# A new opening, a later fourth batch and a fourth buffer for scaled q in a cosformer-attention and expert-mixture kernel

## The chip, the cores and the metric

The kernel runs on one core of one Trainium2 chip. The metric is device time in microseconds (us) of one execution. Executions are compared within rounds on the same chip; a run over 1.5% above the fastest of its kernel counts as slow and is left out of a ratio. Engines are named as in the profile: PE is the matmul engine, DVE the vector engine, ACT the scalar engine, POOL and SP the two from which the transfers here are issued ("POOLq", "SPq"). A lower-case q at the end of a name in the wait views means that engine's sequencer. The granted PE clock is the share of its full clock that the matmul engine was given: 1.00 is full, 0.50 half.

## The reference

Eight batches of linear attention feed a dense mixture of eight experts, whose weights per token come from eight Sinkhorn iterations. Cut to what matters:

```python
batch, n_heads, seq, head_dim = 8, 8, 576, 64         # q, k, v in float32
q_p = phi(q, cos_w, sin_w)    # relu(q), once times cos and once times sin: 128 features
k_p = phi(k, cos_w, sin_w)
kv  = einsum('bhsf,bhsd->bhfd', k_p, v)
z   = sum(k_p, axis=2)
attn = einsum('bhsf,bhfd->bhsd', q_p, kv) / (einsum('bhsf,bhf->bhs', q_p, z)[..., None] + 1e-06)
x = attn as (4608, 512)                                # tokens by model width
P = sinkhorn(exp(x @ w_gate), 8 rounds)
out = sum over e of P[:, e:e+1] * (relu(x @ w1[e]) @ w2[e])
```

## The kernel before

The first 163 us are the subject. They are cut into blocks. In block j, PE runs the first expert's feed-forward layers for token block j (8 slots of first-layer tiles, 8 of second-layer tiles), and between them, slot by slot, the attention of a later batch: sums of batch j+1 (k times v), its denominators, spreading of reciprocals and numerators. In the same block DVE and ACT prepare batch j+2, and POOL issues the loads of batch j+3.

The pools that the change touches:

```python
ld      = pool("ld", bufs=4)          # loads of q, k, v; every name has its own four buffers
qp_pool = pool("qp_pool", bufs=3)     # q times cos and sin, read by the transpose
rb_pool = pool("rb_pool", bufs=4)     # reciprocals spread over partitions
```

From batch 2 on, scaled q is turned by a DMA transpose that the sync queue issues (four per batch, numbered here (batch, hk), where hk is one of four pairs of heads). A q buffer is free again only when its transpose has landed (DVE stands 1.23 us for one at 82.01, below):

```python
def prep_q(b, hk):
    q16 = loaded.pop(("q", b, hk))
    by_dma = b >= 2
    ...                                               # ReLU on DVE
    q_p = qp_pool.tile([P, C, 2, D], F16, name="q_p")
    ve.tensor_tensor(out=q_p[:], in0=q16..., in1=cs, op=ALU.mult)
    if by_dma:
        qTs[b, hk] = q_pTs[(b * HK + hk) % len(q_pTs)]
        turned = nc.sync.dma_start(out=qTs[b, hk], in_=q_p[:]..., transpose=True)
        if b == 3 and hk == 0:
            after(landing["v", b, 1], turned)         # a wait for the last v load of its batch
```

Loads are issued on POOL. `held_back` makes a load wait for the DVE instruction that stands last before it in the program, so it cannot go out before DVE has come that far:

```python
def load(b, half, names="qkv", held_back=False):
    for name in names:
        x = ld.tile([P, 2, C, D], F16, name=f"{name}_ld")
        i = nc.gpsimd.dma_start(out=x[:]..., in_=view[:, 2 * half : 2 * half + 2])
        if held_back:
            after(ve.last, i)
```

The table that deals work to slots, cut to blocks 1 and 2 and the loads:

```python
(4, prep_q, 0), (5, prep_q, 1), (8, prep_k, 0), (8, prep_q, 2), (9, prep_k, 1), (10, prep_kv, 0), ...   # j == 1
(4, prep_q, 0), (5, prep_k, 0), (5, prep_q, 1), (6, prep_k, 1), (8, prep_q, 2), ... (11, prep_kv, 0)    # j == 2
if j == 1:
    at(j, 15, sums, b + 1, 0)
    at(j, 12, load, b + 2, half, name, True)          # batch 4: all six loads
elif j and b + 2 < B:
    at(j, 11 + half, load, b + 2, half, "qkv", True)  # batches 5 to 7: behind DVE's v copy of (b+1, 0)
```

`prep_kv` is the scaled product of k and the copy of v.

## Time and profile before

| | |
|---|---|
| time | 975.6 us median of 3 (975.55 to 975.99) |
| profiled run, one more | 973.88 us, span 972.1 us, mean granted PE clock 0.999 |
| PE busy | 959.4 us, so 12.7 us idle |
| starts of blocks 1, 2, 3 and 4 on PE | 44.86, 67.08, 85.62, 104.65 us |

Each row of a timeline gives start, length, engine, source line (a helper's), operation, what is written and read, and in brackets how long the engine had been idle and what ended that. For a DMA the length is that of its issue, not of its transfer. First the sync queue, asked for batch 4's four transposes one by one:

```profile
76.03 1.61 SPq L392 DMA_TRANSPOSE q_pT<-q_p  x1
77.75 3.07 SPq L392 DMA_TRANSPOSE q_pT<-q_p  x1
80.92 1.31 SPq L392 DMA_TRANSPOSE q_pT<-q_p  x1
82.83 1.27 SPq L392 DMA_TRANSPOSE q_pT<-q_p  x1
```

DVE at the last of them, POOL at the first of batch 5's loads, and the landing of the fourth transpose:

```profile
82.01 0.76 DVE L109 TENSOR_TENSOR q_p<-q_ld,acc_hi 128x1152 f16<-128x1152 f16 x1 [1.23 <-DMA q_pT<-q_p]
...
83.35 0.45 DVE L109 COPY acc_lo<-v_ld 128x576 f16<-128x576 f16 x1
```

```profile
84.10 0.72 POOL L233 DMA_DIRECT2D q_ld<-in_q_dram  x1 [13.47 <-DVE acc_lo L109]
```

```profile
DMA to landing us min/median/max: 4.2/4.2/4.2
```

What to see: with three buffers the fourth product of q has to wait until the first transpose has landed (1.23 us). DVE's v copy comes after that product, and it is the v copy that releases batch 5's loads (84.10). So the fourth transpose (82.83) is out 1.27 us ahead of them, and it lands in 4.2 us. And PE in block 3, from the denominators of batch 4 to the first spread of block 3:

```profile
91.43 0.84 PE L109 MATMUL small_ps<-q_pT,zsel 128*32 128x192 f16 x24
92.20 1.04 PE L109 MATMUL h_ps<-xT,w1e 128*128 128x512 f16 x4
93.07 0.65 PE L109 MATMUL small_ps<-wg,xT 128*128 128x8 f16 x20
93.58 1.89 PE L109 MATMUL h_ps<-xT,w1e 128*128 128x512 f16 x8
95.30 0.41 PE L109 MATMUL small_ps<-hl,acc_hi 96*128 96x192 f16 x3
```

### The profile page before, as it was taken

The numbers are of one execution on the slowest core, as the hardware profiler recorded it, in microseconds if no ns is written. First come the engines' busy times: TensorE is split into PE (matmuls) and PEld (weight loads), VectorE is DVE, ScalarE is ACT, GpSimd is POOL, SyncE is SP. The second block draws the span as 40 slices with busy tenths as digits, with TensorE's granted clock in tenths as the row PEclk, the third lists the DMA queues.
The fourth block names the chain that finished last, engine by engine and source line by source line (L and its number), as shares of the span: only waits on it lengthen the run. The fifth ranks groups of instructions, "written<-read, shape, count | busy, mean of one in ns | idle before, by whom it ended". The sixth has DMA issues, their size and how long they took to land.

```text
span 972.1 us, 20258 instructions
## 1 busy us (share of the span) xinstructions
PE 959.4 (99%) x7855; PEld 674.6 (69%) x7855; DVE 807.4 (83%) x1831; ACT 565.0 (58%) x1264; POOL 60.7 (6%) x82
## 2 busy tenths in 40 slices
PE   9999999999999999999999999999999999999997
PEld 6545555567777777777777777777777777777775
DVE  7767776789898887987888987987888987987887
ACT  5767665577776555555555555555555555555551
POOL 6231210010000000000000000000000000000001
PEclk9999999999999999999999999999999999999999
DMA  9999988231004301332004301322004401115435
GB/s 162 188 154 173 156 137 184 44 69 50 26 26 93 69 25 50 68 62 57 25 26 93 69 25 51 68 54 65 26 25 86 75 25 42 33 28 124 123 90 127
DMA packets 81200, 74.72 MB, mean 77 GB/s; under 512 B 33360, under 2 KB 73040, under 8 KB 81104
## 3 DMA queue, kind: packets, MB, share of 16 engines
q0 software_dynamic: 27232, 30.94, 20.4%
q1 hardware_dynamic: 53632, 42.24, 17.8%
q8 instruction: 61, 1.00, 0.4%
q14 instruction: 35, 0.29, 0.1%
q10 hardware_dynamic: 240, 0.26, 0.1%
HBM read 84.30 MB, written 12.98 MB: 100 GB/s over the span
## 4 chain that ended last, share of the span: by engine, by line
PE 91%; DMA 4%; issue 2%; DVE 1%; POOL 1%; ACT 0%; POOLq 0%; DVEq 0%; SPq 0%; ACTq 0%
PE rows_ps L109 34%; PE h_ps L109 28%; PE p_ps L109 11%; PE copied_ps L109 11%; PE y_ps L109 4%; PE small_ps L109 3%; DMA k_ld<-in_k_dram 1%; DMA w1e<-in_moe_w_dram 1%; DMA w2e<-in_moe_w_dram 1%; DVE acc_hi L975 0%; POOL q_ld L233 0%; POOL hs_last L990 0%; DMA out_dram<-acc_lo 0%; DVE H L905 0%; DVE S L203 0%
## 5 line engine op out<-in xcount | busy, mean ns | idle before, releaser
L975 DVE SCALAR_TENSOR_TENSOR acc_lo<-rows_ps,P_tok,acc_lo 128x512 f32<-128x512 f32 (+1 forms) x322 | 203.8, 642 | 74.9 <-PE rows_ps L109 74.8
L109 PEld LDWEIGHTS <-H 128*128 128x128 f16 x2080 | 203.1, 98 | 82.3 <-issue 1.4
L911 ACT CAST u<-h_ps 128x384 f16<-128x384 f32 x288 | 137.5, 478 | 129.7 <-PE h_ps L109 129.7
L109 PEld LDWEIGHTS <-w1e 128*128 128x128 f16 x1632 | 157.7, 98 | 67.2 <-issue 5.3
L905 DVE CUSTOM_DVE_ANT_0 H<-p_ps,u 128x384 f16<-128x384 f32 x329 | 181.7, 552 | 7.2 <-PE p_ps L109 7.1
L109 PEld LDWEIGHTS <-hs 128*128 128x128 f16 x1500 | 146.6, 98 | 56.2
L109 PE MATMUL p_ps<-xT,T 128*128 128x384 f16 x672 | 164.2, 326 | 1.0 <-DVE H L905 0.9
L109 PE MATMUL h_ps<-S,w1e 128*128 128x384 f16 x672 | 164.2, 326 | 0.8 <-ACT u L911 0.6
L109 PE MATMUL rows_ps<-V,H 128*128 128x256 f16 x1000 | 150.0, 273 | 0.7 <-DVE acc_hi L975 0.7
L109 PE MATMUL rows_ps<-w2e,hs 128*128 128x256 f16 x1000 | 150.0, 273 | 0.0
L109 PE MATMUL h_ps<-xT,w1e 128*128 128x384 f16 (+1 forms) x616 | 148.8, 351 | 0.1
L943 ACT ACTIVATE H<-h_ps 128x384 f16<-128x384 f32 x144 | 70.6, 490 | 94.5 <-PE h_ps L109 94.5
L109 PEld LDWEIGHTS <-T 128*128 128x128 f16 x1008 | 98.4, 98 | 31.9 <-issue 4.9
L109 PE MATMUL rows_ps<-w2e,H 128*128 128x256 f16 (+1 forms) x568 | 94.4, 285 | 0.0
L924 ACT COPY copied_ps<-h_ps 128x384 f32<-128x384 f32 x144 | 67.5, 469 | 36.0 <-PE h_ps L109 35.2
L934 ACT ACTIVATE H<-copied_ps 128x384 f16<-128x384 f32 x144 | 70.8, 492 | 20.4 <-PE copied_ps L109 20.4
L109 PE MATMUL h_ps<-S,T 128*128 128x384 f16 x336 | 81.8, 325 | 0.6 <-ACT copied_ps L109 0.5
L109 PE MATMUL copied_ps<-xT,w1e 128*128 128x384 f16 x336 | 82.1, 326 | 0.0
L109 PE MATMUL copied_ps<-w2e,H 128*128 128x256 f16 x504 | 75.6, 273 | 0.0
L109 PE MATMUL rows_ps<-V,hs 128*128 128x256 f16 x500 | 75.0, 273 | 0.0
L975 DVE SCALAR_TENSOR_TENSOR acc_lo<-copied_ps,P_tok,acc_lo 128x256 f32<-128x256 f32 x126 | 60.3, 479 | 0.4
L975 DVE SCALAR_TENSOR_TENSOR acc_hi<-rows_ps,P_tok,acc_hi 128x512 f32<-128x512 f32 (+1 forms) x56 | 41.4, 739 | 20.6 <-PE rows_ps L109 19.7
(146 smaller groups left out, 947.7 us busy)
## 6 DMA issues: line engine op xcount, KB each, us to landing
S<-x_saved SPq DMA_DIRECT2D x114, 192.0 KB, 2.4
out_dram<-acc_lo SPq DMA_DIRECT2D x62, 128.0 KB, 2.4
w1e<-in_moe_w_dram POOLq DMA_DIRECT2D x7, 1024.0 KB, 8.8
w2e<-in_moe_w_dram POOLq DMA_DIRECT2D x7, 1024.0 KB, 9.6
q_ld<-in_q_dram POOLq DMA_DIRECT2D x16, 288.0 KB, 6.5
k_ld<-in_k_dram POOLq DMA_DIRECT2D x16, 288.0 KB, 7.8
v_ld<-in_v_dram POOLq DMA_DIRECT2D x16, 288.0 KB, 9.6
x_saved<-S SPq DMA_DIRECT2D x12, 192.0 KB, 1.8
```

Source lines behind the costliest of these rows:

```text
L109: i = getattr(self.engine, name)(*args, **kwargs)
L905: latest = ve._custom_dve(TENSOR_ADD_SAT, out=out, in0=ps[:, 0:TU], in1=t[:], s0=FP32_MAX, s1=0.0)
L911: se.copy(out=t[:], in_=ps[:, 0:TU])
L924: se.copy(out=Y[:, 0:TU], in_=X[:, 0:TU])
L934: se.activation(out=h11, in_=Y[:, 0:TU], func=AF.Relu)
L943: se.activation(out=h12, in_=X[:, 0:TU], func=AF.Relu)
L975: ve.scalar_tensor_tensor(out=a, in0=rows, scalar=P_tok[:, g, self.e : self.e + 1], in1=a, op0=ALU.mult, op1=ALU.add,)
```

## The change

The intent: shorten the opening, where PE runs fillers; take away the wait of PE at 59 us on ACT; let scaled q of a batch go ahead without waiting for its own transposes (a fourth buffer, paid with one of the reciprocals'); and keep the DMA transposes of batch 3 away from its loads, by holding them for v and holding batch 4's loads for the transposes. The core of the diff, with cuts marked:

```diff
-        qp_pool = ... bufs=3            # scaled q
+        qp_pool = ... bufs=4
-        rb_pool = ... bufs=4            # reciprocals
+        rb_pool = ... bufs=3
-        def load(b, half, names="qkv", held_back=False):
+        def load(b, half, names="qkv", held_back=False, behind=None):
-                if held_back:
+                if behind is not None:
+                    after(turnings[behind], i)
+                elif held_back:
                     after(ve.last, i)
 # opening
         load(0, 0, "q")
+        load(0, 1, "q")
         ...iota...
+        load(0, 0, "k")
         ...
-        load(0, 1, "q")
-        for name in "kv":
-            load(0, 0, name)
-            load(0, 1, name)
+        load(0, 1, "k")
+        for half in range(2):
+            load(0, half, "v")
 ... (filler of half width; memsets moved ahead; all k products behind the key sums;
 ...  spreads and numerators of batch 0 between the first feed-forward matmuls;
 ...  half of the sums of batch 3 moved from the end of block 1 into block 2)
 # transposes of batch 3
-                if b == 3 and hk == 0:
+                if b == 3:
                     after(landing["v", b, 1], turned)
+                turnings[b, hk] = turned
 # block 1 and block 2
-                    (4, prep_q, 0), (5, prep_q, 1), (8, prep_k, 0), (8, prep_q, 2),
-                    (9, prep_k, 1), (10, prep_kv, 0), (10, prep_k, 2), (12, prep_q, 3),
-                    (12, prep_kv, 1), (12, prep_k, 3), (13, prep_kv, 2), (14, prep_kp, 3), ...
+                    (4, prep_q, 0), (5, prep_q, 1), (9, prep_k, 0), (8, prep_q, 2),
+                    (10, prep_k, 1), (12, prep_q, 3), (12, prep_k, 2), (13, prep_k, 3),
+                    (13, prep_kv, 0), (14, prep_kv, 1),
-                    (4, prep_q, 0), (5, prep_k, 0), (5, prep_q, 1), (6, prep_k, 1),
-                    (8, prep_q, 2), (8, prep_k, 2), (10, prep_q, 3), (10, prep_k, 3), ...
+                    (5, prep_q, 0), (6, prep_q, 1), (8, prep_k, 0), (8, prep_q, 2),
+                    (9, prep_k, 1), (10, prep_q, 3), (10, prep_k, 2), (11, prep_k, 3), ...
-                if j == 1:
-                    at(j, 15, sums, b + 1, 0)
-                        at(j, 12, load, b + 2, half, name, True)
+                        at(j, 12, load, b + 2, half, name, True, (b + 1, HK - 1))
```

## The prediction

> **What bounds the kernel now.** I read the page's first and fourth parts, then PE's own waits in the opening 90 us, then time-ordered views of PE, DVE and ACT where PE waits, and last the landings of the DMA transposes.
>
> ```profile
> PE 959.4 (99%) x7855; PEld 674.6 (69%) x7855; DVE 807.4 (83%) x1831; ACT 565.0 (58%) x1264; POOL 60.7 (6%) x82
> PE 91%; DMA 4%; issue 2%; DVE 1%; POOL 1%; ACT 0%; POOLq 0%; DVEq 0%; SPq 0%; ACTq 0%
> ```
>
> PE is busy in 959.4 of 972.1 us, so all idle PE time together is 12.7 us, 1.3% of the span. No reordering can win 2% (19.5 us) unless it also removes PE work. What is left is idle time and filler matmuls in the opening. PE's waits between 20 and 90 us:
>
> ```profile
> PE small_ps L109 <- ACT rb L109: 1.1, 1, 1.1
> PE small_ps L109 <- ACT acc_lo L109: 0.7, 1, 0.7
> PE small_ps L109 <- ACT q_pT L109: 0.4, 1, 0.4
> PE small_ps L109 <- DVE acc_hi L109: 0.3, 1, 0.3
> ```
>
> From about 86 us the stretches are full. In order of time on PE:
>
> ```profile
> 1.14 5.72 PE L109 MATMUL y_ps<-ones_sq 128*128 128x128 f16 x74 [1.14 <-DVE ones_sq L109]
> 7.65 0.34 PE L109 MATMUL small_ps<-ident,q_p 128*128 128x128 f16 x3 [0.29 <-DVE q_p L109]
> 16.54 1.15 PE L109 MATMUL y_ps<-ones_sq 128*128 128x512 f16 x5
> 17.67 0.42 PE L109 MATMUL small_ps<-hl,acc_hi 96*128 96x192 f16 x3
> 32.82 1.03 PE L109 MATMUL small_ps<-acc_lo,k_p 64*128 64x65 f16 x54 [0.73 <-ACT acc_lo L109]
> 33.78 1.04 PE L109 MATMUL y_ps<-w2e,hT 128*128 128x512 f16 x4
> 59.48 0.46 PE L109 MATMUL small_ps<-hl,acc_hi 96*128 96x192 f16 x3 [1.11 <-ACT rb L109]
> ```
>
> Matmuls on ones_sq are filler: they look busy, but PE is waiting. So up to 17.67 us the end is set by loads and DVE, not by PE. The DVE chain there:
>
> ```profile
> 4.32 0.50 DVE L109 COPY cs_half<-acc_hi 64x18 f16<-64x18 f16 x2 [1.39 <-ACT acc_hi L109]
> 6.83 0.77 DVE L109 TENSOR_TENSOR q_p<-q_ld,acc_hi 128x1152 f16<-128x1152 f16 x1
> 10.50 0.53 DVE L109 TENSOR_SCALAR k_ld<-k_ld 128x576 f16<-128x576 f16 x2 [1.57 <-DMA k_ld<-in_k_dram]
> 15.50 1.35 DVE L109 RECIPROCAL den<-y_ps 96x192 f32<-96x192 f32 x1
> ```
>
> The gap at 59.48 starts on ACT, which stands on a ReLU of the fourth batch's k until its load lands, with a copy to rb behind it:
>
> ```profile
> 57.89 0.68 ACT L109 ACTIVATE k_ld<-k_ld 128x576 f16<-128x576 f16 x1 [2.25 <-DMA k_ld<-in_k_dram]
> 58.48 0.57 ACT L109 COPY acc_lo<-y_ps 128x512 f32<-128x512 f32 x1
> 58.95 0.70 ACT L109 COPY rb<-small_ps 128x384 f32<-128x384 f32 x2
> ```
>
> [...] here sixteen take 3.59 us from 44.86, or 224 ns[...]. [...] the transpose issued at 53.64 us amid the batch's loads landed after 10.2 us, the one at 63.16, after the last v, after 3.3 us.
>
> **The change part by part.**
>
> Opening. The second q load and one k load are issued ahead of the other set-up work, so the index row is some 0.75 us later (one load's issue on POOL is 0.72 to 0.87 us). The two sines follow and end near 5.05 us instead of 4.29. But DVE now does its memsets (0.43 for the mask, about 0.4 for the rest) in the wait it had (1.39 us), and the cs_half copies (0.50) come after two q products. Then come the row reduction, select and spread (5.34 to 6.60 before), so the first q product starts at about 6.1 instead of 6.83. The four q products and the copies end at about 9.5, ahead of k, whose first half landed at 10.48 and, issued slightly earlier, may land at 10.2.
>
> From k's landings: ReLU of two k tiles 0.52; the second pair lands at about 11.9 and is ready near 12.5; key sums on PE 0.75, to 13.3; DVE's scaled k product (0.7) overlaps; mask product 0.3, to 13.75; denominators 0.5, to 14.35; one k product to 14.4; reciprocal 1.35, cast and remainder 0.7: about 16.5. Before, two more k products lay ahead of the reciprocal, and it ended at 17.60. Gain here 1.1 us, and the filler ahead (18 quarters before, 20 after) still covers the wait.
>
> From there PE runs four spreads and four numerators (0.36 each), the second half of the sums (0.65) and sixteen feed-forward matmuls (3.45), about 7.4 us with small filler: the next feed-forward tile starts at about 24.0 instead of 24.98.
>
> Then DVE binds. The changed order puts all four k products of batch 1 behind the last xT product (about 23.0); DVE had done two of them in its gaps before. Work from there: 4 k products and 4 q products at 0.69 (5.5), 2 ReLUs (0.6), 4 evictions of turned q at 0.46 (1.85), and 4 v copies at 0.38 (1.5), of which ACT did two before. That is 9.5 us, to 32.5; sums follow, and the second-layer tile starts at about 33.0 instead of 33.78. So of 1.1 us about 0.75 survives.
>
> Block 1 (second token block), where batch 2 is attended. The ReLU of k of batch 3 (the fourth batch) goes one slot later, behind the first attend. The rb copy then finds ACT free. PE needs, between 58.20 and 60.54, only 0.72 us for the spread and numerators that it took 2.34 us for: gain 1.62 us. The first half of the batch's sums (0.67 us at 66.41) moves into the next block, neutral. The scaled k and v copies move behind it: from about 64.3 DVE has 4 times 1.07 us to do, ending near 68.4; the sums in slot 2 reach the fourth tile at about the same time: at most 0.2 us.
>
> Block 2. All four transposes of this batch now wait for v (before, one of them went early, 53.64). With steps of 1.4 us from 62.0 and 3.4 to land, the last lands near 69.7, and batch 4's loads, which went out at 66.33, wait for that. An unhindered first load took 4.8 us (issued 84.1), so q is in at about 74.5. DVE reaches its first q product at 73.4 and stands about 1.1 us; three of them (1.0 each) end at 77.65, ahead of two xT products that free the accumulators of the third spread, due on PE at 77.75. The first is free at about 78.1: a loss of 0.4 to 0.6 us, taken as 0.5.
>
> The buffers: a fourth scaled q means its product doesn't wait for the transpose three products back (only 1.2 us of such DVE wait in the whole trace); three reciprocals suffice, since no more than two are outstanding when the next spread starts. Nothing for either. From block 3 on, order and engines' work are the same.
>
> Sum: 0.75 + 1.62 - 0.5 = 1.87, so 975.6 - 1.9 = 973.7 us.
>
> **Rivals.**
> (a) The later loads of batch 4 give it all back. For it: q, k and v land 2 to 3 us later than before, and ACT's ReLUs of k come ahead of output copies. Against: k moves from slots 5, 6, 8, 10 to 8 to 11[...]. If block 2 loses 2 us: 975.2 us.
> (b) The DVE queue of the opening isn't the bound I make it and all 1.1 us, or more, survives. Before, PE lost 0.40, 0.35 and 0.73 us at 29 to 33 us, part to ACT's v copies, now gone. Against: DVE's 9.5 us has no slack in my count. If right, with 1 us more: 972.6 us.
> [...]
> (d) A mere shift: the opening's gain is eaten by batch 2's loads (landing 36 to 43 us). Against: their issue waits only for earlier transfers and buffers, and PE is full from 33.78 to 44.86. It would leave 1.1 us: 974.5 us.
>
> **Range and chances.** The opening may bring 0.3 to 1.8, block 1 1.2 to 1.7, block 2 from 0.2 gained to 1.8 lost. Adding one bad term to otherwise central ones gives 971.5 to 975.5 us for 8 in 10. Faster by over 2% would need more idle time than there is: 0.01. Slower by over 2% would need a new wait of 19 us: 0.005. Within 2%: 0.985.
>
> **What would show it.** In the changed profile: first q product on DVE near 6.1; remainder done near 16.5; PE without waits from there to about 26, then two waits of 0.3 to 0.7 us on DVE among the turned q tiles; second-layer tile near 33.0. The 1.11 us wait on rb gone, and the 2.25 us ACT idle with it. All transposes of the fourth batch after v, 3 to 4 us each, then q loads near 69 (less the shift of 0.75); a DVE wait on q of about 1 us and a PE wait of about 0.5 us near 77. From block 3 on, everything the same but earlier by 1.9 us. I am wrong if PE shows a new wait of over 1 us in blocks 1 to 3, or if the second-layer tile starts before 32.3 or after 33.6.

Cut from it is what no trace of this case had shown: statements on the matmul clock, on matmul rates (the "sixteen" left standing are 512-column matmuls), on the order of work on ACT and on transfer engines; the second argument against rival (a); and rival (c), on the clock in the opening. That a block's feed-forward matmuls are a floor rested on the second and was not shown. No term of the sum is cut: 0.75 + 1.62 - 0.5 = 1.87 us, so 973.7 us.

## The result, and the profile after

The changed kernel took 983.77 us (median of 4, 981.29 to 984.21), the kernel before 975.63 us (975.55 to 975.99). The ratio is 1.0077, with a 95% interval of 1.006 to 1.0095; here and below a ratio is the mean time of one kernel's fast runs over the mean of the other's fast runs in the same rounds, so not quite the ratio of the medians quoted. The kernel became 0.8% slower: within the 2% that counts as the same, but slower where a small gain, to 973.7 us, had been predicted.

The profiled run took 984.03 us, with a span of 982.3 us. Busy time, from the page:

```profile
PE 961.8 (98%) x7886; PEld 674.9 (69%) x7886; DVE 808.9 (82%) x1834; ACT 564.0 (57%) x1261; POOL 60.4 (6%) x82
```

PE is busy 2.4 us longer (961.8 against 959.4) and idle 7.8 us longer (20.5 against 12.7); together that is the 10.2 us that the span grew. (The medians are only 8.1 us apart: the profiled run of the kernel before, 973.88 us, was faster than its median.) The first two blocks did what the change was for: PE starts blocks 1, 2 and 3 at 43.64, 63.40 and 84.04 us, that is 1.22, 3.68 and 1.58 us earlier than before (0.67 us of the 3.68 is work that was moved from block 1 to block 2). But block 4 starts at 114.59, 9.94 us later than before. So nearly everything that was lost was lost in block 3. The longest of PE's waits between 20 and 125 us (waited for: us in total, times, longest); the others are of 0.4 us and less:

```profile
PE small_ps L109 <- DMA q_pT<-q_p: 8.5, 2, 8.3
...
```

PE in order of time, the same work as in the lines of before from 91.43 to 95.30:

```profile
90.01 0.51 PE L109 MATMUL small_ps<-q_pT,zsel 128*32 128x192 f16 x12
90.75 0.35 PE L109 MATMUL small_ps<-q_pT,zsel 128*32 128x192 f16 x6 [0.22 <-DMA q_pT<-q_p]
99.36 0.51 PE L109 MATMUL small_ps<-q_pT,zsel 128*32 128x192 f16 x6 [8.27 <-DMA q_pT<-q_p]
99.81 1.89 PE L109 MATMUL h_ps<-xT,w1e 128*128 128x512 f16 x4
101.49 0.72 PE L109 MATMUL small_ps<-wg,xT 128*128 128x8 f16 x20
102.07 3.34 PE L109 MATMUL h_ps<-xT,w1e 128*128 128x512 f16 x8
105.24 0.41 PE L109 MATMUL small_ps<-hl,acc_hi 96*128 96x192 f16 x3
```

Two losses stand in these lines. The last quarter of batch 4's denominators waits 8.27 us for a transposed q. And the twelve feed-forward matmuls behind that wait take nearly twice as long: with the gate matmuls between them, from the row at 99.81 to the spread at 105.24 it is 5.43 us, where before it was 3.10 us (92.20 to 95.30). The stretches of 5 us show why; the columns are the stretch, busy time of PE, PEld, DVE, ACT and POOL, the granted PE clock, and the DMA share and rate:

```profile
95.00:100.00 5.00, 0.64 (x7) 0.27 (x7) 0.09 (x1) 0.00 (x0) 0.00 (x0) 0.50 0.80 131
100.00:105.00 5.00, 5.00 (x31) 2.04 (x30) 4.79 (x10) 1.31 (x3) 0.00 (x0) 0.50 0.07 14
```

The clock fell to half during the wait and stayed there until about 105 us: the trace's clock records have 0.50 from 94.79 to 105.03 us. PE had waited 8.27 us, and while the clock is 0.50 there is a 512-column matmul every 0.42 us (99.81 to 101.49 is four of them) instead of every 0.22 (92.20 to 93.07 in the kernel before, at 1.00). Block 3 is 11.52 us longer than before (30.55 against 19.03): 8.49 of waits, 2.33 of half-clock matmuls, and 0.70 spread over the denominators and the sums.

Why did the transpose come so late? The sync queue, transpose by transpose, and POOL's first load of batch 5:

```profile
74.80 2.50 SPq L403 DMA_TRANSPOSE q_pT<-q_p  x1
77.41 5.95 SPq L403 DMA_TRANSPOSE q_pT<-q_p  x1
83.46 1.60 SPq L403 DMA_TRANSPOSE q_pT<-q_p  x1
85.17 2.36 SPq L403 DMA_TRANSPOSE q_pT<-q_p  x1
```

```profile
83.50 0.72 POOL L234 DMA_DIRECT2D q_ld<-in_q_dram  x1 [10.01 <-DVE acc_lo L109]
```

The landing of the fourth transpose, asked for that transpose alone:

```profile
DMA to landing us min/median/max: 14.2/14.2/14.2
```

And DVE at the product and the copy that stood at 82.01 and 83.35 before:

```profile
78.47 0.76 DVE L109 TENSOR_TENSOR q_p<-q_ld,acc_hi 128x1152 f16<-128x1152 f16 x1
...
82.75 0.45 DVE L109 COPY acc_lo<-v_ld 128x576 f16<-128x576 f16 x1 [2.85 <-DMA v_ld<-in_v_dram]
```

The reader is to see an order that turned round. Batch 4's loads go out at 69.18 to 72.73 instead of 66.33 to 69.88, so its transposes are issued among them; the issue of the second alone occupies the sync queue for 5.95 us. DVE no longer notices: with a fourth buffer it makes its fourth q product at 78.47 without waiting for any transpose, and goes on to the v copy, which v's own landing (82.72) holds until 82.75. That copy releases batch 5's six loads at 83.50, while the third transpose is just being issued and the fourth has 1.7 us to go. The fourth goes out at 85.17 among these loads. The six land between 88.96 and 99.20 us, the fourth transpose at 99.32. With no loads in flight a transpose lands in 3.3 to 3.7 us (the first three of batch 3, issued at 60.58 to 63.41, land 3.31 to 3.37 us later, the fourth, issued at 64.91, 3.7 us later).

So the theory is: a transpose that is issued behind the first of a batch's loads lands late, in the change only when the last of the six has landed (the third transpose, issued 0.04 us ahead of the first of them, landed at 90.70); before, three buffers kept the transpose ahead of the next batch's loads without anybody having asked for it; the fourth buffer took that away. The rivals: that the hold on batch 4's loads alone does it, by making everything of batch 4 late; that the new order of work does it; and that the half clock has another cause than the wait.

### The profile page after: what moved, and what is told of

Read it like the earlier page. It is cut to its first block, busy times and chain, and to the rows that moved or that the text cites. A ratio compares the mean times of both kernels' runs of the same rounds, so it can differ in the third digit from the quotient of the medians.

```text
span 982.3 us, 20307 instructions
## 1 busy us (share of the span) xinstructions
PE 961.8 (98%) x7886; PEld 674.9 (69%) x7886; DVE 808.9 (82%) x1834; ACT 564.0 (57%) x1261; POOL 60.4 (6%) x82
## 4 chain that ended last, share of the span: by engine, by line
PE 93%; DMA 3%; DVE 2%; ACT 1%; issue 1%; POOL 0%; POOLq 0%; ACTq 0%; DVEq 0%; SPq 0%
PE rows_ps L109 34%; PE h_ps L109 28%; PE p_ps L109 11%; PE copied_ps L109 11%; PE y_ps L109 5%; PE small_ps L109 3%; DMA q_pT<-q_p 1%; DMA k_ld<-in_k_dram 1%; ACT q_pT L109 0%; ACT hT L109 0%; DMA acc_hi<-q_p 0%; DVE acc_hi L991 0%; ACT acc_lo L109 0%; POOL hs_last L1006 0%; DMA out_dram<-acc_lo 0%
## 5 line engine op out<-in xcount | busy, mean ns | idle before, releaser
L109 PE MATMUL h_ps<-xT,w1e 128*128 128x384 f16 (+1 forms) x616 | 150.9, 355 | 0.1
```

Source lines behind the costliest of these rows:

```text
L109: i = getattr(self.engine, name)(*args, **kwargs)
```

## The experiments

All eighteen kernels gave correct results. They ran in five calls, each with its own runs of the kernel before, which scatter too: its medians were 976.83, 975.51, 975.61, 975.88 and 975.00 us, with single runs up to 981.3. So the ratios are what is to be compared across calls.

### The hold and the buffer, each undone

`e1_no_hold`: the changed kernel, batch 4's loads not held for the last transpose of batch 3.

```diff
-  at(j, 12, load, b + 2, half, name, True, (b + 1, HK - 1))
+  at(j, 12, load, b + 2, half, name, True)
```

> The changed kernel with one part undone: the loads of the fifth batch (batch 4) no longer wait for the last transpose of batch 3; they are released as in the kernel before. Theory A (the held loads start at 69.2 us, 5.8 us into block 2, so that batch 4's own transposes run among its v loads and the next batch's loads, and the fourth lands at 99.4): the wait of 8.3 us on a transpose in block 3 goes, and so does the half clock after it. Then the time is 972 to 975 us, unless the same collision now falls on batch 3's transposes, whose sums are due at 69.4 us: a wait of 1 to 4 us there would make it 974 to 978. Theory B (the fourth buffer lets a transpose too many be outstanding) and theory C (the later slots of the batch-4 q products in block 2): the 8.3 us wait stays within 2 us, time 981 to 984.

Measured: 983.67 us (982.82 to 985.31), ratio 1.0063 [1.0029, 1.0096]. As slow as with the hold. The wait went from block 3 to block 2:

```profile
78.67 0.51 PE L109 MATMUL small_ps<-acc_lo,zsel 128*32 128x192 f16 x6 [9.00 <-DMA acc_lo<-q_p]
```

Batch 3's third transpose was issued at 63.48 amid batch 4's loads (62.17 to 65.72) and landed at 78.62, 0.01 us after the last of them. In the new order it is DVE's fourth q product that releases batch 4's loads when they are not held (61.88), and with four buffers it waits for no transpose. The hold does protect batch 3; without it, the same overtaking happens one batch earlier. So the hold by itself is not the loss.

`e2_hold_alone`: the kernel before with nothing but the hold (and the record of transposes that it needs).

```diff
+  turnings[b, hk] = turned
-  at(j, 12, load, b + 2, half, name, True)
+  at(j, 12, load, b + 2, half, name, True, (b + 1, HK - 1))
```

> The kernel before with only the hold added. There block 2 starts at 67.1 us and the last transpose of batch 3 would land near 69.5, so the loads go out about 3.2 us later than in the kernel before, but only 2.4 us into the block (5.8 in the changed kernel). Theory A: the slack that the kernel before had, 4.4 us between the last landing of a transpose (87.0) and its use (91.4), is mostly used up: 0 to 4 us lost, 976 to 980 us. If the hold alone is the whole cause: 984 us or more. Theories B and C: no loss, 975 to 976 us.

Measured: 978.83 us (978.04 to 979.96), ratio 1.0011 [0.9984, 1.0038], not distinguishable from before. No wait on a transpose in the profile. In the old order of block 2, k is due early, and its late load shows as PE waits of 2.11 and 0.45 us behind ACT at 80.60 and 81.65.

`e3_three_q`: the changed kernel with the fourth q buffer taken back.

```diff
-  qp_pool ... bufs=4
+  qp_pool ... bufs=3
```

> The changed kernel with three buffers for scaled q instead of four. Theory B: with one transpose fewer outstanding, the wait of 8.3 us in block 3 shrinks by half or more, time under 979 us. Theory A: the loads are still as late, DVE now stands before the fourth q product until the first transpose has landed (85.2 us), so block 2 gets a new wait of some us and block 3 keeps one: 983 to 990 us.

Measured: 976.96 us (976.05 to 978.51), ratio 0.9992 [0.9964, 1.002]. The hold and the new order remain and the loss is gone. DVE's row of the fourth q product shows what brings it back into order:

```profile
85.10 0.76 DVE L109 TENSOR_TENSOR q_p<-q_ld,acc_hi 128x1152 f16<-128x1152 f16 x1 [4.00 <-DMA q_pT<-q_p]
```

DVE stands 4.00 us until the first transpose has landed; the v copy comes behind it (86.45), batch 5's loads at 87.19, and by then the fourth transpose is out (85.92, landed 3.2 us later).

`e11_no_hold_three_q`: both undone, the fourth corner of the square.

```diff
-  qp_pool ... bufs=4
+  qp_pool ... bufs=3
-  at(j, 12, load, b + 2, half, name, True, (b + 1, HK - 1))
+  at(j, 12, load, b + 2, half, name, True)
```

> The changed kernel with both undone, the hold and the fourth q buffer; with the runs that undo one of them it makes the square. Theory (with three buffers DVE stands until a transpose has landed, so a later load can't pass the fourth): no PE wait on a transpose above 1 us, in block 2 or in block 3, full clock, and small waits of DVE and PE in block 1 as with three buffers and the hold: 975 to 977.5 us. Rival (the new order of blocks 1 and 2 itself makes loads pass transposes): a wait of over 4 us as without the hold and with four buffers, 981 us or more.

Measured: 974.7 us (973.55 to 976.53), ratio 0.9988 [0.9974, 1.0002], a little under the expected range. The square, as ratios to the kernel before of the same rounds:

| | four q buffers | three q buffers |
|---|---|---|
| with the hold | 1.0077 (the change) | 0.9992 (`e3_three_q`) |
| without | 1.0063 (`e1_no_hold`) | 0.9988 (`e11_no_hold_three_q`) |

With this order of work the buffer decides: 0.75 to 0.85% or 7 to 8 us either way. The hold decides only in which block the wait falls. The rival "the hold alone" falls, and so does "the new order alone".

### Who overtakes whom: fixing the order

`e4_hold_all`: the changed kernel, loads of every later batch also held for the last transpose of the batch ahead.

```diff
-  at(j, 11 + half, load, b + 2, half, "qkv", True)
+  at(j, 11 + half, load, b + 2, half, "qkv", True, (b + 1, HK - 1))
```

> The changed kernel with the same hold on every later batch too: batch 5's loads wait for the last transpose of batch 4, and so on. Theory A, in its second half (the fourth transpose is slow because batch 5's loads, issued from 83.5 us, come in among the transposes): the third and fourth transposes land at 87 to 91 us instead of 90.7 and 99.4, the wait in block 3 shrinks to under 2 us; each later block may get the small waits of block 2 (0.9 us), so 973 to 978 us. If only batch 4's own loads are the trouble: the fourth transpose still lands after 94, and the wait stays over 4 us, in every block perhaps, 985 us or more.

Measured: 980.55 us (978.39 to 981.06), ratio 1.0023 [0.9995, 1.0052]. The wait on the transpose is gone (batch 4's land at 85.37 to 88.96), but batch 5's loads go out at 89.5, its k lands at 95.94, and PE waits 4.34 us for ACT, which has the ReLU of k ahead of an output of the feed-forward; the clock falls to half again. A hold that is too long buys one wait with another.

`e6_next_held`: the changed kernel, only batch 5's loads held, for batch 4's second transpose.

```diff
-  at(j, 11 + half, load, b + 2, half, "qkv", True)
+  at(j, 11 + half, load, b + 2, half, "qkv", True, (b + 1, 1) if j == 2 else None)
```

> The changed kernel with batch 5's loads alone released by the landing of batch 4's second transpose instead of by DVE's v copy. Theory (the fourth transpose is late because batch 5's loads go out ahead of it): it now goes out first and lands at about 89 to 91 us; the wait for it falls below 0.5 us; the first k of batch 5 lands at about 92.5, which may cost PE about 1 us behind ACT; no half clock; 973.5 to 976.5 us. Rival (the late loads of batch 4 alone slow its transposes): the wait stays above 4 us and the time above 981 us.

Measured: 976.96 us (976.03 to 977.72), ratio 1.0006 [0.9979, 1.0032]. The transpose goes out at 85.59 ahead of the loads (87.16) and lands at 88.91, and its wait is gone: the loads of the next batch were the cause, not the lateness of batch 4's own. The cost was mis-sized: k landed at 94.08 instead of the expected 92.5, and PE waited 2.85 us behind ACT, not 1.

`e7_half_hold`: the changed kernel, batch 4's loads held for batch 3's second transpose instead of the fourth, so that batch 4 is earlier.

```diff
-  at(j, 12, load, b + 2, half, name, True, (b + 1, HK - 1))
+  at(j, 12, load, b + 2, half, name, True, (b + 1, 1))
```

> The changed kernel with batch 4's loads held behind the second transpose of batch 3 instead of the fourth, so they are out some 3.5 us earlier and land some 3 us earlier. Theory (order decides: with four buffers the v copy, and with it batch 5's loads, comes ahead of the fourth transpose however early batch 4 is): batch 5's loads still precede the fourth transpose, and PE still waits 4 to 8 us for it, with half clock: 979 to 984 us. Rival (only how late batch 4's loads are matters): the wait is gone, 972 to 975 us.

Measured: 980.88 us (979.77 to 983.15), ratio 1.0048 [1.0023, 1.0074]. Batch 4's loads went out 66.45 to 70.01, about as in the kernel before, and still batch 5's (80.09) passed the fourth transpose (82.11, landed 95.38, the last load at 95.39); PE waited 6.2 us. An early batch 4 is not enough.

`e8_both`: the last two together.

> Both together: batch 4's loads behind batch 3's second transpose, batch 5's behind batch 4's second. Theory: [...] no wait above 1.5 us in blocks 1 to 4, full clock; the gains of the opening and of block 1 (about 2.8 us together) survive: 971.5 to 974 us. Rival (batch 3's last two transposes, or k of batch 5, are late instead): a wait of over 3 us in block 2 or 4, 977 us or more.

Measured: 973.17 us (971.39 to 974.71), ratio 0.9966 [0.9941, 0.9991]: 0.3% faster than the kernel before, and near the 973.7 us that the prediction had named for the change. Batch 4's fourth transpose is out at 81.27 and lands in 3.2 us, batch 5's loads follow at 82.78. PE's longest wait from 20 to 125 us is 0.51 us:

```profile
PE h_ps L109 <- ACT hT L109: 0.5, 1, 0.5
...
```

`e12_both_three_q`: `e8_both` with three q buffers.

> The mended version (batch 4's loads behind batch 3's second transpose, batch 5's behind batch 4's second) with three q buffers instead of four. Theory: once the order is settled by explicit releases, the fourth buffer is a gain of its own, for with three DVE stands 3 to 4 us for a transpose in block 1 with accumulators to free behind it: 975 to 977 us against some 973.2 with four. Rival (the buffer is worth nothing): 972.5 to 974 us.

Measured: 973.94 us (973.48 to 974.32), ratio 0.9979 [0.9966, 0.9993]. My theory, that the fourth buffer is then a gain of its own of 2 us or more, falls. DVE does stand 5.0 us in all for transposes again, and PE shows 1.8 and 1.1 us of small waits from it, yet the time is within the noise of `e8_both`. Once the order is asked for, the buffer does no harm, and no gain from it is shown.

### The half clock

`e5_filler`: the changed kernel with 36 filler matmuls of 512 columns ahead of batch 4's denominators.

> The changed kernel with 36 filler matmuls of 512 columns put on PE just ahead of the denominators of batch 4, where it stood idle for 8.27 us. Theory (the long idle wait is what halves the PE clock for the 10 us after it, worth about 2.4 us): the idle wait shrinks to about 1 us or less, the granted clock stays full at 95 to 105 us, and the kernel takes about 981.5 us (980.5 to 982.5), though the transpose still lands at about 99.3. Rival (the slow matmuls after the wait have another cause, or the filler costs as much as it saves): 983 to 985 us.

Measured: 982.28 us (980.5 to 986.9), ratio 1.007 [1.004, 1.0099], inconclusive. The three runs with a mean clock of 0.999 or more took 980.5, 981.51 and 981.51 us, where the theory had put them; the three with 0.998 took 983.04, 986.19 and 986.9. The profiled run is the worst of them: there batch 5's loads (83.89) passed two transposes, the last landed at 103.19, and even with the filler PE waited 3.88 us and its clock fell. That the wait causes the half clock is supported by every profile with a PE wait of over 4 us on a transpose and no filler (8.27 us in the change, 9.00 in `e1_no_hold`, 6.2 in `e7_half_hold`, 4.8 and 7.5 in `e14_this_held`, 7.7 in `e15_both_held`, 6.6 and 4.3 in `e16_opening_both`, each with stretches of 5 us at a clock of 0.50 after it began), and by none against it; this run does not settle it further.

The clock records say more. In the traces of the kernel before and of the change, all changes of the granted clock lie whole multiples of 3.41 us behind the first record (at 3.95 and 6.04 us): 283 of them before; 26, 29 and 286 in the change, whose half-clock stretch lasts 10.24 us. In the stretches of 5 us the other profiles show half clock for about 3.4 us (`e5_filler`: 0.95 and 0.71 from 100 to 110) and 6.8 us (`e2_hold_alone`: 0.55 and 0.77 from 80 to 90; `e4_hold_all`: 0.98, 0.50 and 0.83 from 90 to 105; `e7_half_hold`: 0.89, 0.50 and 0.93 from 90 to 105). The two traces were cut into windows of 3.41 us from the first clock record on, and PE's idle time was added up in each. While the clock was full, it fell at the end of each of the three windows with 1.99 us of idle time or more (1.99 us before, at the end of the program; 3.41 us in the change, once in the wait and once at the end), and of none with 1.78 us or less. So it is the wait that halves the clock, whoever ends it: in `e4_hold_all` ACT did, after 4.34 us, with the clock at 0.50 from 95 to 100. The length of the wait alone does not decide: after the 2.85 us in `e6_next_held` (92.47 to 95.32) the clock stayed at 1.00, while with a wait of 2.11 us in `e2_hold_alone` (0.55 from 80 to 85) and one of 2.3 us in `e15_both_held` (0.89 from 105 to 110) it fell. That it depends on where a wait lies among the windows is the author's estimate, not shown by a run.

### The parts on the kernel before

`e9_opening`: the kernel before with the new opening alone.

> The kernel before with the new opening alone (everything up to and with the first token block), the rest as before: three q buffers, no hold, the old order of blocks 1 and 2. Theory: the gain of 1.2 us at the second-layer tile stays to the end, the 1.1 us wait on rb and the order of transposes and loads are as before: 973.5 to 975 us where the kernel before takes 975.5. Rival (the opening's shift alone upsets a later order): a PE wait of over 2 us in blocks 1 to 4, 977 us or more.

Measured: 973.07 us (972.35 to 977.31), ratio 0.9981 [0.9964, 0.9998]. The second-layer tile starts at 32.45 instead of 33.78 and the gain lasts to the end. The opening is a gain as predicted. But the order in block 2 is close here too: batch 3's last transpose went out 0.10 us ahead of batch 4's first load, PE waited 1.07 us for it, and one of the six runs took 977.31 us at a clock of 0.995.

`e10_before_four_q`: the kernel before with nothing but the buffers changed.

```diff
-  qp_pool ... bufs=3        rb_pool ... bufs=4
+  qp_pool ... bufs=4        rb_pool ... bufs=3
```

> The kernel before with nothing but the buffers changed (four of scaled q, three of reciprocals). Theory (the buffer does harm only where batch 4 is late enough for the sync queue to be blocked): DVE's 1.23 us wait at 82 us is gone, batch 5's loads go out about 1.2 us earlier, at about 82.9 us, still just behind the fourth transpose at about 82.3: within 1 us of before, 975 to 976.5 us. Rival (the buffer alone is the harm): the loads go ahead of the fourth transpose, PE waits 4 us or more for it, 979 us or more.

Measured: 978.17 us, but from 973.1 to 984.32; ratio 1.0027 [0.9992, 1.0061]. The six runs with their mean clocks: 973.1 (0.999), 973.68 (1.000), 977.38 (0.998), 978.97 (0.998), 983.48 (0.994), 984.32 (0.995). Neither theory nor rival had this: one program, two outcomes. The profiled run (973.68) is a good one. In it the order is kept by little: batch 3's last transpose is issued at 66.16 and batch 4's first load at 66.34. The slow runs have the clock of the changed kernel, but no profile.

So in three more steps the order was to be fixed on this kernel. `e13_next_held`, `e14_this_held` and `e15_both_held` hold, on `e10_before_four_q`, batch 5's loads for (4,1), batch 4's for (3,1), and both; `e16_opening_both` adds the new opening to the last.

```diff
-  at(j, 12, load, b + 2, half, name, True)
+  at(j, 12, load, b + 2, half, name, True, (b + 1, 1))                            # e14, e15, e16
-  at(j, 11 + half, load, b + 2, half, "qkv", True)
+  at(j, 11 + half, load, b + 2, half, "qkv", True, (b + 1, 1) if j == 2 else None)   # e13, e15, e16
```

> The kernel before with four q buffers, and batch 5's loads released by the landing of batch 4's second transpose. If the scatter comes from block 3 (batch 5's loads overtaking batch 4's fourth transpose): all runs within 972.5 to 976 us with a clock of 0.998 or more. If it comes from block 2 (batch 4's loads overtaking batch 3's fourth transpose): runs over 980 us with a clock of 0.996 or less remain.

Measured: 986.32 us median, from 974.31 to 990.41, of which the two slowest count as slow; ratio of the rest 1.0039 [0.9988, 1.0089]. The scatter stays, but this does not show that block 2 makes it, because the hold did not fix block 3. Even in the profiled run, a good one, it lets batch 5's first load out 0.21 us behind the fourth transpose, where `e10_before_four_q` without any hold had 1.27 us (82.20 and 83.47):

```profile
82.86 1.27 SPq L395 DMA_TRANSPOSE q_pT<-q_p  x1
```

```profile
83.07 0.72 POOL L234 DMA_DIRECT2D q_ld<-in_q_dram  x1 [12.47 <-DMA q_pT<-q_p]
```

> The kernel before with four q buffers, and batch 4's loads released by the landing of batch 3's second transpose. If the scatter comes from block 2: all runs within 972.5 to 976 us. If from block 3: runs over 980 us with a clock of 0.996 or less remain. A profile that shows one of them shows a PE wait of over 5 us on a transposed q.

Measured: 986.8 us (986.02 to 987.95), ratio 1.0106 [1.0085, 1.0127]. This is neither expectation, and the fault was mine. PE's waits:

```profile
PE small_ps L109 <- DMA acc_hi<-q_p: 7.5, 1, 7.5
PE small_ps L109 <- DMA acc_lo<-q_p: 4.8, 1, 4.8
```

In the compiled program of the kernel before, the sync queue has transpose (3,1) ahead of (3,0): only (3,0) waits for v, and the one that goes out first in the trace does not. So (3,1) lands at 64.76 at the end of batch 3's own loads, and a hold on it lets batch 4's loads out at 65.29, ahead of the last two transposes (65.55 and 67.32, landed 77.51 and 85.54, 18.2 us after issue). As a test of which block scatters it is void. As a test of the mechanism it is the plainest of all: put the loads ahead of two transposes, here by mistake, and PE waits 12.3 us for them.

> Both holds on the kernel before with four q buffers. Theory (the scatter is loads overtaking transposes, in whichever block): all six runs within 972.5 to 975.5 us, clock 0.998 or more. Rival (the scatter has another cause, such as the chip's other traffic): runs over 977 us remain.

Measured: 992.14 us (990.8 to 994.09), ratio 1.0159 [1.0136, 1.0181], with the same fault: waits of 7.7 and 3.3 us on batch 3's transposes. A third wait, of 2.3 us on batch 4's last, comes from the other hold: (4,1) landed at 92.82 and let batch 5's loads out at 93.39, 2.05 us ahead of the fourth transpose (95.44).

> The same with the new opening. Theory: its 1.2 us add to the former: 971.5 to 974 us, some 1.2 us below the kernel with both holds and the old opening, no PE wait above 1.2 us in blocks 1 to 4. Rival (the opening's gain is lost as the order is now fixed by landings): no faster than that kernel.

Measured: 989.46 us (986.33 to 990.25), ratio 1.0123 [1.0099, 1.0146], both faults again.

`e17_both_mended` and `e18_opening_mended` are the last two with the holds on (3,0), which is the second that is issued, and on (4,2).

```diff
-  (b + 1, 1)                      # of batch 4's loads
+  (b + 1, 0)
-  (b + 1, 1) if j == 2 else None  # of batch 5's loads
+  (b + 1, 2) if j == 2 else None
```

> The kernel before with four q buffers and both orders really fixed: batch 4's loads behind transpose (3,0), the second of batch 3 to be issued (lands at about 66.6 us, after the fourth's issue at 66.2), batch 5's behind (4,2). Theory (the scatter is loads overtaking transposes): all runs within 972.5 to 975.5 us, clock 0.998 or more, no PE wait on a transpose over 1.2 us. Rival (another cause): runs over 977 us remain.

Measured: 974.17 us, six runs from 973.88 to 974.86; ratio 0.9986 [0.9969, 1.0002]. With the same buffers as `e10_before_four_q`, whose runs spread over 11.2 us, these spread over 1.0 us. In its profile the loads follow the last transpose by 0.92 us in block 2 and by 2.92 us in block 3. This supports that the scatter was loads overtaking transposes; no slow run was profiled, so it has not been seen.

> The same with the new opening. Theory: its 1.2 us add: 971.5 to 974 us, about 1.2 us below the kernel of the other run, no PE wait above 1.2 us in blocks 1 to 4. Rival (the gain is lost now that landings fix the order): no faster than the other run.

Measured: 972.85 us (971.92 to 973.08), ratio 0.997 [0.9952, 0.9988], 1.3 us below `e17_both_mended` in the same rounds. Its longest PE wait between 20 and 125 us is 0.5 us. This and `e8_both` are the best versions found, not distinguishable from one another: 0.3% below the kernel before and 1.1% below the change.

Not settled: in which block the slow runs of `e10_before_four_q` lost their time. In its good profile block 2 is the closer one (0.18 us against 1.27), but `e13_next_held` and `e14_this_held`, meant to tell the two apart, both failed to fix the order that they were to fix. Nor was any of the single runs of the kernel before at 979 to 981 us profiled, so whether its own close order in block 2 (66.08 against 66.33) is sometimes lost is a guess.

## Why the prediction was wrong

Step by step, with the predicted values first:

- Opening. First q product 6.1, measured 6.07; remainder done 16.5, measured 16.2; next feed-forward tile 24.0, measured 23.77; second-layer tile 33.0, measured 32.55. The gain was 1.23 us instead of 0.75. The mechanism was right; the term "So of 1.1 us about 0.75 survives" was too small; the time lay between it and rival (b). `e9_opening` shows that the gain lasts to the end.
- Block 1. Gain 1.62 us; the block shortened by 2.46, of which 0.67 is moved work, so 1.79. The wait on rb is gone. Right.
- Block 2. Loss 0.5 us; the block grew by 2.10, of which 0.67 is moved work, so 1.43. q landed at 73.61 (74.5 predicted), DVE stood 0.91 us for it (1.1). PE's waits are 0.18, 0.36 and 0.36 us, 0.9 in all. There was a loss, but nearly three times the size, and mostly on another path than the one worked out: only the first wait is DVE's; the other two are for copies of ACT, which had stood 2.75 us for batch 4's k (78.06). That path is the one that rival (a) names.
- Up to here the sum was 1.87 us and block 3 did start 1.58 us earlier. The step that failed is the last one: "Nothing for either [buffer]. From block 3 on, order and engines' work are the same." The order of work on the engines is the same, but the order between two queues was not on any engine's list: the fourth transpose on the sync queue and batch 5's loads on POOL. Block 3 cost 11.52 us more.
- The sentence on the fourth buffer took the 1.23 us DVE wait that it removes for idle time that costs nothing. That wait was what kept the loads behind the transpose. The square of four runs (7 to 8 us for the buffer, nothing for the hold) shows it.
- Rival (a) came nearest to the place, the later loads of batch 4. But its second argument against, that k's loads are clear of the transposes, was untrue: batch 4's k loads (out at 70.61, landed at 79.45) were in flight together with batch 4's own transposes (issued at 74.80 and 77.41, landed 10.4 and 8.8 us later). And it stopped at 2 us because it looked for the cost in late q, k and v, not in late transposes.
- The prediction had the decisive fact in hand. It quoted a transpose issued amid loads that landed after 10.2 us, and one alone that took 3.3 (issued at 63.20, not 63.16 as it has it), and used it for batch 3 alone.
- "I am wrong if PE shows a new wait of over 1 us in blocks 1 to 3" was the right test; it was met at 99.36 us.
- Half clock after a long wait (0.50 from 94.79 to 105.03) was in no term of the forecast; rival (c) asked about the clock in the opening only. It added 2.3 us here.

With the order fixed, `e8_both` took 973.17 us, where 973.7 was predicted for the change. That the totals agree is partly luck. It is another kernel, with another hold, and term by term its profiled run gained 1.75 us in the opening and 1.80 in block 1 (without the moved work), gained 0.13 in block 2 where 0.5 was to be lost, and lost 0.96 in block 3.

## What to carry to other kernels

A wait that costs nothing may still be what holds two queues in order: before adding a buffer, ask what the engine that no longer waits will release earlier, and what on another queue it can then overtake. Where a transfer with a near deadline must precede bulk loads, write that dependence down, on the transfer itself and on the right one in the compiled order, rather than rely on a buffer count. And when one program's runs fall into two groups with different clocks, suspect an order that is decided by a few tenths of a microsecond.

## What the traces showed of transposes and the clock

- A transpose among loads: issued at 85.17 among six loads that landed until 99.20 it landed at 99.32 (14.2 us; all six loads were issued within 1.9 us of it); likewise 63.48 to 78.62 with the last load at 78.61 (`e1_no_hold`), and 82.11 to 95.38 with 95.39 (`e7_half_hold`). It does not always land so late: in `e14_this_held` one issued at 65.55 landed at 77.51, while transfers went on (162 GB/s from 80 to 85 us) and the next transpose landed at 85.54. With no loads in flight one took 3.3 to 3.7 us (batch 3 of the change). Why it lands so late, no run here shows.
- The order of transposes and loads was worth 7 to 8 us here.
- A transpose's issue took 1.29 to 1.33 us with no loads in flight (batch 3 of the change, 60.58 to 64.91), but 5.95 us (the change, 77.41), 5.87 us (`e14_this_held`, 67.32) and 8.39 us (`e5_filler`, 86.3) among loads; in the change the next transpose went out only 0.1 us after its end.
- The full clock came back 5.67 us after PE went on in the change (99.36 to 105.03), and about 7.3 us after in `e1_no_hold` (78.67 to about 85.9, from a clock of 0.91 in the stretch from 85 to 90; with a wait of 0.42 us in it).
